# Two linear-attention blocks on one core: the denominators summed by partition copies on ScalarE and additions on VectorE instead of matmuls

## The chip, the core and the metric

The kernel runs on one core of one Trainium2 chip. The metric is the device time of one execution in microseconds; less is better. The engines are named as in the profile: PE is TensorE (PEld its weight loads), ACT is ScalarE, DVE is VectorE, POOL is GpSimd, SP is SyncE, which only issues DMAs. All of them run at the same time, each through its own list of instructions in program order, and semaphores make them wait for one another.

## What is computed

Two blocks, A and B, with their own inputs, do the same work; their outputs stand side by side. For each:

```
qkv = x @ wqkv                      # x: 2048 x 640, wqkv: 640 x 1920, 32 heads of 20
phi(t) = (t + 1 if t > 0 else exp(t)) + 1e-6
pq, pk = phi(q), phi(k)
kv  = einsum("bhsd,bhse->bhde", pk, v)
z   = einsum("bhsd->bhd", pk)
num = einsum("bhqd,bhde->bhqe", pq, kv)
den = einsum("bhqd,bhd->bhq", pq, z) + 1e-6
out = (num / den, heads concatenated) @ wo
```

All of it is fp32. For each token and head, `den` is one number: the sum over the head's 20 dimensions of pq times z.

## The kernel before

**Accuracy.** TensorE multiplies in a reduced fp32 form. Each operand is therefore split into a high part (a copy on ScalarE) and a low part (source minus high part, on VectorE), and a product is three matmuls: high by high, high by low, low by high. A helper `split` issues the copy at once and puts the subtraction on a list; `flush` (called at every slot, see below) issues what is on the list.

**First half (to about 313 us).** It makes phi(k) and, in place of kv, the products of phi(k) with x, from which kv and its product with wo follow (640 x 640, one per block). It is ordered by a small planner in the kernel. The change doesn't touch it.

**Second half.** The 2048 tokens of each block are cut into 4 units of 512 tokens, so there are 8 units (u = 0 to 7). Two stages work on a unit:

- the projection (`qmm`, `qphi`, `qacc`): five column blocks c = 0 to 4 of q, transposed, so that 128 columns of q lie on the partitions and 512 tokens in the free dimension. Each takes 15 matmuls of 512 columns into a bank `psq`. ScalarE takes the exponential (eq, L1092) and the ReLU (rq, L1093) from the bank, VectorE combines them to pq (L1094), and pq times z is added up over the five blocks in `acc` (128 x 512; first block on ScalarE, L1102, the others on VectorE, L1104). The columns of q are ordered by dimension first and head second, so partition p belongs to head p mod 32, and the four groups of 32 partitions of acc still have to be summed.
- the output (`outmm`): 14 steps s = 0 to 13, 108 matmuls of 320 columns. They compute pq/den times the combined 640 x 640 matrix by a scheme with 7 products for each of two halves q of the unit. The products use two banks `pa` and two `pe`, and `psb`. A bank pa is copied out by ScalarE (L1218) after steps 0 and 1, again after 4 and 5, after 8 and 9, and after 10 and 11, and between these the next product is added to the same bank. So the matmuls of step 4 wait for the copy of step 0, and those of step 10 for the copy of step 8.

The stages run in the order q0, q1, o0, q2, o1, q3, ..., q7, o6, o7.

**The denominators before.** `split_acc` splits acc into a high and a low part (ScalarE L918, VectorE L915), `denmm` multiplies both with `same`, a 128 x 128 matrix that is 1 where two partitions belong to the same head (two matmuls of 512 columns, L1114 and L1115, into the bank `psd`). All 128 partitions then hold the sum of their head. `recip` takes the reciprocal on VectorE in two halves of 256 tokens (L1120), and `divide` multiplies one half of pq by it (VectorE, L1126). Then `d_sums` forms sums and differences of parts of pq (sr, L1142 to L1147), and `a_split` and `d_split` split these into the high and low operands of `outmm` (da and ds).

**What sets the order.** It is written out by hand. `run("q", u, c, k)` is called after each three matmuls of the projection and `run("o", u, s)` after each step of the output; `at(slot, f, ...)` puts a function into such a slot. The dict `chain` holds the slots of the denominator's functions for each unit v. Those of unit 0 lie in the projection of unit 1, those of unit v > 0 in the output stage of unit v - 1. As each engine works in program order, a slot decides behind which other instruction a function's instructions stand. In the projection, `qphi` of block c comes after all five slots of that block. In the output, a step's own copies come before its slot. Around the slots stand, among others, the splits of wo of block B (woh and wol, in the projection of unit 1), the rounding of the next x (xqh, L962, slots 4, 6, 8, 10 and 12 of an output stage) and the splits of block B's matrix (fsh, in the output stage of unit 0 and others).

Of the kernel before, what the change touches and what calls it, by code (L numbers as in the profile page):

```python
# [7 lines left out]
F32 = mybir.dt.float32  # L8
BF16 = mybir.dt.bfloat16
F32R = mybir.dt.float32r  # L10
I32 = mybir.dt.int32
AF = mybir.ActivationFunctionType
OP = mybir.AluOpType
# [205 lines left out]
def tile_linear_attn_pair(ctx: ExitStack, tc: tile.TileContext, ins, out: bass.AP):  # L219
    nc = tc.nc  # L220
    P = 128
# [19 lines left out]
    kx, kg, q1a, q1b, q2, q3 = [], [], [], [], [], []  # L241
# [19 lines left out]
    same = base.tile([P, P], F32R)  # L261
# [415 lines left out]
    a, z, x = jh[0][0:P], jl[0][0:P], jr[0][0:P]  # L677
# [117 lines left out]
    for p in range(4, NPB):  # L795
        i, h = divmod(p - 2, 2)
# [9 lines left out]
    for p in range(NPB + 1, NP):  # L806
        if p == NPB + 1:
            fl = kvs
        else:
            i, h = divmod(p - NPB - 2, 2)  # L810
# [70 lines left out]
    for g, (h0, nh) in enumerate(GROUPS):  # L881
        cols = NC * DH * nh
        w = Space("wv", cols, (BD,))
# [17 lines left out]
    def bank(name, tag="one", bufs=3):  # L901
        at, n = ptags[tag]
        pn[tag] = pn.get(tag, -1) + 1
        return psum.tile([P, 512], F32, name=name, tag=f"bank{at + pn[tag] % n}", bufs=1)
# [7 lines left out]
    def flush():  # L912
        while lows:
            lo, src, hi = lows.pop(0)
            nc.vector.tensor_tensor(lo, src, f32(hi), op=OP.subtract)  # L915

    def split(hi, lo, src, now=False):
        nc.scalar.activation(hi, src, AF.Copy)  # L918
        lows.append((lo, src, hi))
        if now:  # L920
            flush()
# [148 lines left out]
    pq, acc, den, dd = {}, {}, {}, {}  # L1070
# [32 lines left out]
        else:  # L1103
            nc.vector.scalar_tensor_tensor(acc[u], p, z, acc[u], op0=OP.mult, op1=OP.add)  # L1104

    def split_acc(u):
        t = q2[0].tile([P, 2, 512], F32R, name="ac", tag="sr", bufs=2)
        split(t[:, 0], t[:, 1], acc.pop(u))
        acc[u] = t

    def denmm(u):
        t = acc.pop(u)
        ps = den.pop(u) if u in den else bank("psd", "small", 1)
        nc.tensor.matmul(ps, same, t[:, 0], start=True, stop=False)  # L1114
        nc.tensor.matmul(ps, same, t[:, 1], start=False, stop=True)  # L1115
        den[u] = (ps, q2[0].tile([P, 512], F32, name="rd", tag="rd", bufs=1))

    def recip(u, h):
        ps, r = den[u]
        nc.vector.reciprocal(r[:, h * 256:(h + 1) * 256], ps[:, h * 256:(h + 1) * 256])  # L1120

    def divide(u, h):

# [4 lines left out]
    da, ds, sr = {}, {}, {}  # L1128
# [161 lines left out]
    h = NG - 1  # L1290
# [8 lines left out]
    for c in range(NC):  # L1299
# [3 lines left out]
        for u in range(1, NU - 1):  # L1303
# [3 lines left out]

    at(("q", 1, 0, 0), z_end)

    den[0] = bank("psd", "small", 1)  # L1310

    chain = {
        0: [(("q", 1, 0, 0), split_acc, 0), (("q", 1, 1, 1), denmm, 0), (("q", 1, 1, 1), recip, 0, 0),
            (("q", 1, 1, 1), recip, 0, 1), (("q", 1, 1, 2), divide, 0, 0), (("q", 1, 1, 4), divide, 0, 1),
            (("q", 1, 2, 0), d_sums, 0, 0), (("q", 1, 2, 2), a_split, 0, 0), (("q", 1, 2, 4), d_sums, 0, 1),
            (("q", 1, 3, 1), d_split, 0, 0), (("q", 1, 3, 4), a_split, 0, 1), (("q", 1, 4, 1), d_split, 0, 1)]}
    for v in range(1, NU):
        w, u = v - 1, v + 1
        if v == NU - 1:
            chain[v] = [(("o", w, 1), split_acc, v), (("o", w, 4), denmm, v), (("o", w, 4), recip, v, 0),  # L1320
                        (("o", w, 5), divide, v, 0), (("o", w, 6), a_split, v, 0, 0), (("o", w, 6), d_sums, v, 0, 0),
                        (("o", w, 7), d_split, v, 0, 0), (("o", w, 8), a_split, v, 1, 0), (("o", w, 8), d_sums, v, 1, 0),
                        (("o", w, 9), recip, v, 1), (("o", w, 10), d_split, v, 1, 0), (("o", w, 12), divide, v, 1),
                        (("o", v, 0), a_split, v, 0, 1), (("o", w, 13), d_sums, v, 0, 1),
                        (("o", v, 0), d_split, v, 0, 1), (("o", v, 2), d_sums, v, 1, 1),
                        (("o", v, 2), a_split, v, 1, 1), (("o", v, 3), d_split, v, 1, 1)]
        elif v == 1:
            chain[v] = [(("o", w, 4), split_acc, v), (("o", w, 7), denmm, v), (("o", w, 8), recip, v, 0),
                        (("o", w, 10), recip, v, 1), (("o", w, 11), divide, v, 0),
                         (("o", w, 12), divide, v, 1), (("q", u, 0, 2), d_sums, v, 0), (("q", u, 0, 4), a_split, v, 0),  # L1330
                         (("q", u, 1, 2), d_sums, v, 1), (("q", u, 2, 1), d_split, v, 0), (("q", u, 3, 1), a_split, v, 1),
                         (("q", u, 3, 4), d_split, v, 1)]
        else:
            chain[v] = [(("o", w, 2), split_acc, v), (("o", w, 5), denmm, v), (("o", w, 7), recip, v, 0),
                        (("o", w, 9), recip, v, 1), (("o", w, 11), divide, v, 0),
                         (("o", w, 12), divide, v, 1), (("q", u, 0, 2), d_sums, v, 0), (("q", u, 0, 4), a_split, v, 0),
                         (("q", u, 1, 2), d_sums, v, 1), (("q", u, 2, 1), d_split, v, 0), (("q", u, 3, 1), a_split, v, 1),
                         (("q", u, 3, 4), d_split, v, 1)]
    for v in range(NU):
        for a, f, *x in chain[v]:  # L1340
            at(a, f, *x)
# [63 lines left out]
```

## Time and profile before

| | us |
|---|---|
| median of 3 runs | 570.86 (570.66 to 571.42) |
| the profiled execution | 570.49 |
| its span, from its first to its last instruction | 568.7 |
| TensorE busy | 564.2 |
| VectorE busy | 434.2 |
| ScalarE busy | 341.4 |

The granted TensorE clock is 1.000 over the span. A row of the timeline reads: start in us, duration in us, engine, line, operation, output tile <- input tiles, shape, how many, and in brackets how long the engine sat idle before it and for whom it waited. A row of a group reads: line, engine, operation, tiles, shape, count, then busy us, mean ns of one, and idle us before them. Matmuls overlap, so the cost of one in a dense stream is the distance of two starts, not its duration.

### The profile page before, as it was taken

Reading aid. Unit: us, or ns where it says so; the run is one execution under the profiler, and the core shown is the slowest. Engines: PE = TensorE matmul, PEld = TensorE weight load, DVE = VectorE, ACT = ScalarE, POOL = GpSimd, SP = SyncE. Lnnn points to the kernel's source line nnn. Section 1 sums busy time; section 2 is a strip of 40 time slices with the busy share of each in tenths; the row PEclk is TensorE's granted clock in tenths of the full one; section 3 lists DMA queues with packets and bytes.
Section 4 is the critical chain, followed back from the end, with each engine's and each line's share of the span. In section 5 each row is a group of like instructions: output and inputs, shape, how many; then the busy total and the mean of one; then the engine's idle time right before and its main releaser. Section 6 shows DMA issues by size and latency. Waiting matters only on the chain.

```text
span 568.7 us, 9488 instructions
## 1 busy us (share of the span) xinstructions
PE 564.2 (99%) x3524; PEld 536.0 (94%) x3524; DVE 434.2 (76%) x706; ACT 341.4 (60%) x619; POOL 62.9 (11%) x103
## 2 busy tenths in 40 slices
PE   9999999999999999999999999999999999999997
PEld 7999999999999999999988899898989989898997
DVE  6888687598888767888645899977788776758792
ACT  6878566673788756766436665646656464644551
POOL 0210011110001021110010103110011201001010
PEclk9999999999999999999999999999999999999999
DMA  8993755758849676697999967662454996122022
GB/s 294 370 283 118 198 150 125 238 142 248 262 116 274 180 190 181 199 295 202 352 281 342 355 238 258 228 193 95 146 202 144 366 391 224 42 76 93 0 93 92
DMA packets 68321, 117.64 MB, mean 207 GB/s; under 512 B 6804, under 2 KB 30132, under 8 KB 68276
## 3 DMA queue, kind: packets, MB, share of 16 engines
q1 hardware_dynamic: 59060, 89.94, 48.0%
q0 software_dynamic: 8928, 26.92, 17.0%
q8 instruction: 27, 0.44, 0.3%
q10 hardware_dynamic: 288, 0.20, 0.1%
q14 instruction: 18, 0.15, 0.1%
HBM read 71.13 MB, written 35.41 MB: 187 GB/s over the span
## 4 chain that ended last, share of the span: by engine, by line
PE 99%; DVE 0%; issue 0%
PE psg L316 25%; PE pa L1203 12%; PE ka L316 10%; PE psq L924 8%; PE psq L926 8%; PE psq L925 8%; PE pe L1203 6%; PE ke L316 5%; PE psk L719 4%; PE psb L1203 4%; PE kb L316 3%; PE pskv L556 1%; PE pskv L984 1%; PE psm L583 1%; PE psi L647 1%; PE psk L696 1%
## 5 line engine op out<-in xcount | busy, mean ns | idle before, releaser
L316 PE MATMUL psg<-pkl,xnh 128*128 128x320 f32 x320 | 98.9, 309 | 0.0
L316 PE MATMUL psg<-pkh,xnh 128*128 128x320 f32 x320 | 98.8, 309 | 0.0
L316 PE MATMUL psg<-pkh,xnl 128*128 128x320 f32 x320 | 98.5, 308 | 0.0
L924 PE MATMUL psq<-xqh,wh 128*128 128x512 f32 x200 | 78.5, 393 | 0.0
L926 PE MATMUL psq<-xqh,wl 128*128 128x512 f32 x200 | 78.0, 390 | 0.0
L925 PE MATMUL psq<-xql,wh 128*128 128x512 f32 x200 | 77.9, 390 | 0.0
L316 PEld LDWEIGHTS psg<-pkl,xnh 128*128 128x128 f32 x320 | 60.1, 188 | 0.0
L316 PEld LDWEIGHTS psg<-pkh,xnl 128*128 128x128 f32 x320 | 60.1, 188 | 0.0
L316 PEld LDWEIGHTS psg<-pkh,xnh 128*128 128x128 f32 x320 | 60.0, 188 | 0.0
L489 ACT ACTIVATE kt<-ka 128x320 f32<-128x320 f32 x52 | 22.7, 437 | 59.1 <-PE ka L316 59.0
L1218 ACT ACTIVATE o<-pa 128x320 f32<-128x320 f32 x64 | 27.9, 438 | 45.2 <-PE pa L1203 45.0
L406 POOL DMA_DIRECT2D zacc<-ek x32 | 26.6, 840 | 236.1 <-DVE ek L499 173.7
L1094 DVE SCALAR_TENSOR_TENSOR pq<-eq,rq 128x512 f32<-128x512 f32 x40 | 27.7, 691 | 30.7 <-ACT rq L1093 30.6
L537 DVE TENSOR_TENSOR gacc<-psg,gacc 128x320 f32<-128x320 f32 x60 | 29.4, 489 | 23.5 <-PE psg L316 22.5
L1092 ACT ACTIVATE eq<-psq 128x512 f32<-128x512 f32 x40 | 23.9, 597 | 36.9 <-PE psq L926 34.8
L926 PEld LDWEIGHTS psq<-xqh,wl 128*128 128x128 f32 x200 | 37.5, 188 | 7.9
L925 PEld LDWEIGHTS psq<-xql,wh 128*128 128x128 f32 x200 | 37.6, 188 | 7.6 <-DMA xql<-xd 0.2
L924 PEld LDWEIGHTS psq<-xqh,wh 128*128 128x128 f32 x200 | 37.6, 188 | 7.1
L401 ACT ACTIVATE pkh<-ek,epst 128x640 fp32r<-128x640 f32 x32 | 26.5, 828 | 6.9 <-DVE ek L499 6.7
L1203 PE MATMUL pa<-fh,dal 128*128 128x320 f32 x96 | 29.7, 309 | 0.0
L1203 PE MATMUL pa<-fh,dah 128*128 128x320 f32 x96 | 29.7, 309 | 0.0
L1203 PE MATMUL pa<-fl,dah 128*128 128x320 f32 x96 | 29.7, 309 | 0.0
(215 smaller groups left out, 1558.2 us busy)
## 6 DMA issues: line engine op xcount, KB each, us to landing
zacc<-ek POOLq DMA_DIRECT2D x32, 320.0 KB, 4.8
xql<-xd SPq DMA_DIRECT2D x40, 256.0 KB, 5.0
xd<-xl SPq DMA_DIRECT2D x29, 320.0 KB, 3.9
out<-o POOLq DMA_DIRECT2D x28, 320.0 KB, 3.6
xns<-in_A_x SPq DMA_DIRECT2D x16, 320.0 KB, 5.4
xts<-in_B_xt_tiles SPq DMA_DIRECT2D x16, 320.0 KB, 3.6
xns<-in_B_x SPq DMA_DIRECT2D x16, 320.0 KB, 5.8
xqs<-in_A_xt SPq DMA_DIRECT2D x20, 256.0 KB, 5.8
```

What stands on the lines that cost most here:

```text
L316: nc.tensor.matmul(o, a.r, w.r, start=start and k == i == 0, stop=k == n - 1 and i == 2, skip_group_check=True)
L401: note("ACT", n + 110, lambda: act(hi.r, p.f, AF.Identity, bias=epst), [hi], [p, K0.all], by=8.0)
L406: note("POOL", 1.0, lambda: nc.gpsimd.dma_start(z.f, p.f, **kw), [z], [p], dma=1.0 if first else 1.86)
L537: tt(o, BK[k].tile[:, :HF], o, op=OP.add)
L719: nc.tensor.matmul(o[h][:, :HF], x[a].r, w[c][h * HF:h * HF + HF].r, start=c == 0 and i == 0, stop=c == NC - 1 and i == 2, skip_group_chec ...
L924: nc.tensor.matmul(o, whi, xhi, start=first, stop=False)
L925: nc.tensor.matmul(o, whi, xlo, start=False, stop=False)
L926: nc.tensor.matmul(o, wlo, xhi, start=False, stop=last)
L1092: nc.scalar.activation(e, ps, AF.Exp)
L1094: nc.vector.scalar_tensor_tensor(pq[u][:, c, :], e, 1.0, r, op0=OP.min, op1=OP.add)
L1203: nc.tensor.matmul(ps, x, y, start=start and n == i == 0, stop=n == len(terms) - 1 and i == 2, skip_group_check=True)
L1218: copy = lambda x, y: nc.scalar.activation(x, y, AF.Copy)
```

## The change

The four partition groups are summed without TensorE. `fold1` copies on ScalarE the upper 64 partitions of the first 256 tokens to the lower 64, and the lower 64 partitions of the last 256 tokens to the upper 64. `fold2` adds them on VectorE: the lower 64 partitions now hold the first 256 tokens, the upper 64 the last 256. `fold3` swaps on ScalarE groups of 32 partitions within each 64 (four copies), `fold4` adds these and takes one reciprocal of 256 columns on VectorE, and `fold5` copies the result on ScalarE to both halves of the partitions (two copies for each 256 tokens). `divide` and all that follows is the same. So there are ten copies, three additions and one reciprocal per unit in place of one copy, one subtraction, two matmuls and two reciprocals. No bank of PSUM is used for it any more. The slots change with it:

```diff
-    def split_acc(u):
-        t = q2[0].tile([P, 2, 512], F32R, name="ac", tag="sr", bufs=2)
-        split(t[:, 0], t[:, 1], acc.pop(u))
-        acc[u] = t
-
-    def denmm(u):
...
-    def recip(u, h):
-        ps, r = den[u]
-        nc.vector.reciprocal(r[:, h * 256:(h + 1) * 256], ps[:, h * 256:(h + 1) * 256])
+    def fold1(u):
+
+        t = q2[0].tile([P, 2, 512], F32, name="ac", tag="sr", bufs=2)
+        a = acc[u]
+        nc.scalar.activation(t[0:64, 0, 0:256], a[64:128, 0:256], AF.Copy)
+        nc.scalar.activation(t[64:128, 0, 0:256], a[0:64, 256:512], AF.Copy)
+        den[u] = t
+
+    def fold2(u):
+        t, a = den[u], acc.pop(u)
+        for p, c in ((0, 0), (64, 256)):
+            rows = slice(p, p + 64)
+            nc.vector.tensor_tensor(t[rows, 0, 256:512], a[rows, c:c + 256], t[rows, 0, 0:256], op=OP.add)
+
+    def fold3(u, h):
+        t = den[u]
+        for p, q in ((0, 32), (32, 0)):
+            p, q = p + 64 * h, q + 64 * h
+            nc.scalar.activation(t[p:p + 32, 1, 0:256], t[q:q + 32, 0, 256:512], AF.Copy)
+
+    def fold4(u):
+        t = den[u]
+        nc.vector.tensor_tensor(t[:, 1, 0:256], t[:, 0, 256:512], t[:, 1, 0:256], op=OP.add)
+        nc.vector.reciprocal(t[:, 1, 256:512], t[:, 1, 0:256])
+        den[u] = (t, q2[0].tile([P, 512], F32, name="rd", tag="rd", bufs=1))
+
+    def fold5(u, h):
+        t, r = den[u]
+        for p in (0, 64):
+            nc.scalar.activation(r[p:p + 64, h * 256:(h + 1) * 256], t[64 * h:64 * h + 64, 1, 256:512], AF.Copy)
...
-        0: [(("q", 1, 0, 0), split_acc, 0), (("q", 1, 1, 1), denmm, 0), (("q", 1, 1, 1), recip, 0, 0),
-            (("q", 1, 1, 1), recip, 0, 1), (("q", 1, 1, 2), divide, 0, 0), (("q", 1, 1, 4), divide, 0, 1),
+        0: [(("q", 1, 0, 0), fold1, 0), (("q", 1, 0, 2), fold2, 0), (("q", 1, 0, 3), fold3, 0, 0),
+            (("q", 1, 0, 4), fold3, 0, 1), (("q", 1, 1, 1), fold4, 0), (("q", 1, 1, 3), fold5, 0, 0),
+            (("q", 1, 1, 4), fold5, 0, 1), (("q", 1, 1, 4), divide, 0, 0), (("q", 1, 2, 0), divide, 0, 1),
...
-            chain[v] = [(("o", w, 1), split_acc, v), (("o", w, 4), denmm, v), (("o", w, 4), recip, v, 0),
-                        (("o", w, 5), divide, v, 0), (("o", w, 6), a_split, v, 0, 0), (("o", w, 6), d_sums, v, 0, 0),
+            chain[v] = [(("o", w, 1), fold1, v), (("o", w, 2), fold2, v), (("o", w, 3), fold3, v, 0),
+                        (("o", w, 3), fold3, v, 1), (("o", w, 4), fold4, v), (("o", w, 6), fold5, v, 0),
+                        (("o", w, 6), divide, v, 0), (("o", w, 7), a_split, v, 0, 0), (("o", w, 7), d_sums, v, 0, 0),
...
-            chain[v] = [(("o", w, 2), split_acc, v), (("o", w, 5), denmm, v), (("o", w, 7), recip, v, 0),
-                        (("o", w, 9), recip, v, 1), (("o", w, 11), divide, v, 0),
...
+            a = (3, 4, 5, 6, 7, 9, 10) if v == 1 else (2, 3, 4, 5, 6, 8, 9)
+            chain[v] = [(("o", w, a[0]), fold1, v), (("o", w, a[1]), fold2, v), (("o", w, a[2]), fold3, v, 0),
+                        (("o", w, a[3]), fold3, v, 1), (("o", w, a[4]), fold4, v), (("o", w, a[5]), fold5, v, 0),
+                        (("o", w, a[6]), fold5, v, 1), (("o", w, 11), divide, v, 0), (("o", w, 12), divide, v, 1),
```

The slots of `divide` for the units 1 to 6 stay where they were, and those of the sums and splits behind it stay for all units but the last, where some move back by one step.

More of the change, by code (lines that the diff above doesn't have):

```diff
@@ L1104, in qacc @@
             nc.vector.scalar_tensor_tensor(acc[u], p, z, acc[u], op0=OP.mult, op1=OP.add)
-    def split_acc(u):
-        t = q2[0].tile([P, 2, 512], F32R, name="ac", tag="sr", bufs=2)
-        split(t[:, 0], t[:, 1], acc.pop(u))
-        acc[u] = t
-    def denmm(u):
[L1112 to L1116, printed above, removed]
-    def recip(u, h):
-        ps, r = den[u]
-        nc.vector.reciprocal(r[:, h * 256:(h + 1) * 256], ps[:, h * 256:(h + 1) * 256])
+    def fold1(u):
[23 more added lines that the diff above has]
+            nc.scalar.activation(r[p:p + 64, h * 256:(h + 1) * 256], t[64 * h:64 * h + 64, 1, 256:512], AF.Copy)
     def divide(u, h):
@@ L1308, in tile_linear_attn_pair @@
     at(("q", 1, 0, 0), z_end)
-    den[0] = bank("psd", "small", 1)
     chain = {
-        0: [(("q", 1, 0, 0), split_acc, 0), (("q", 1, 1, 1), denmm, 0), (("q", 1, 1, 1), recip, 0, 0),
-            (("q", 1, 1, 1), recip, 0, 1), (("q", 1, 1, 2), divide, 0, 0), (("q", 1, 1, 4), divide, 0, 1),
+        0: [(("q", 1, 0, 0), fold1, 0), (("q", 1, 0, 2), fold2, 0), (("q", 1, 0, 3), fold3, 0, 0),
+            (("q", 1, 0, 4), fold3, 0, 1), (("q", 1, 1, 1), fold4, 0), (("q", 1, 1, 3), fold5, 0, 0),
+            (("q", 1, 1, 4), fold5, 0, 1), (("q", 1, 1, 4), divide, 0, 0), (("q", 1, 2, 0), divide, 0, 1),
             (("q", 1, 2, 0), d_sums, 0, 0), (("q", 1, 2, 2), a_split, 0, 0), (("q", 1, 2, 4), d_sums, 0, 1),
@@ L1319, in tile_linear_attn_pair @@
         if v == NU - 1:
-            chain[v] = [(("o", w, 1), split_acc, v), (("o", w, 4), denmm, v), (("o", w, 4), recip, v, 0),
-                        (("o", w, 5), divide, v, 0), (("o", w, 6), a_split, v, 0, 0), (("o", w, 6), d_sums, v, 0, 0),
-                        (("o", w, 7), d_split, v, 0, 0), (("o", w, 8), a_split, v, 1, 0), (("o", w, 8), d_sums, v, 1, 0),
-                        (("o", w, 9), recip, v, 1), (("o", w, 10), d_split, v, 1, 0), (("o", w, 12), divide, v, 1),
+            chain[v] = [(("o", w, 1), fold1, v), (("o", w, 2), fold2, v), (("o", w, 3), fold3, v, 0),
+                        (("o", w, 3), fold3, v, 1), (("o", w, 4), fold4, v), (("o", w, 6), fold5, v, 0),
+                        (("o", w, 6), divide, v, 0), (("o", w, 7), a_split, v, 0, 0), (("o", w, 7), d_sums, v, 0, 0),
+                        (("o", w, 8), d_split, v, 0, 0), (("o", w, 9), a_split, v, 1, 0), (("o", w, 9), d_sums, v, 1, 0),
+                        (("o", w, 10), fold5, v, 1), (("o", w, 10), d_split, v, 1, 0), (("o", w, 12), divide, v, 1),
                         (("o", v, 0), a_split, v, 0, 1), (("o", w, 13), d_sums, v, 0, 1),
@@ L1326, in tile_linear_attn_pair @@
                         (("o", v, 2), a_split, v, 1, 1), (("o", v, 3), d_split, v, 1, 1)]
[L1327 to L1332, printed above, removed]
-        else:
-            chain[v] = [(("o", w, 2), split_acc, v), (("o", w, 5), denmm, v), (("o", w, 7), recip, v, 0),
-                        (("o", w, 9), recip, v, 1), (("o", w, 11), divide, v, 0),
-                         (("o", w, 12), divide, v, 1), (("q", u, 0, 2), d_sums, v, 0), (("q", u, 0, 4), a_split, v, 0),
-                         (("q", u, 1, 2), d_sums, v, 1), (("q", u, 2, 1), d_split, v, 0), (("q", u, 3, 1), a_split, v, 1),
-                         (("q", u, 3, 4), d_split, v, 1)]
+        else:
+            a = (3, 4, 5, 6, 7, 9, 10) if v == 1 else (2, 3, 4, 5, 6, 8, 9)
+            chain[v] = [(("o", w, a[0]), fold1, v), (("o", w, a[1]), fold2, v), (("o", w, a[2]), fold3, v, 0),
+                        (("o", w, a[3]), fold3, v, 1), (("o", w, a[4]), fold4, v), (("o", w, a[5]), fold5, v, 0),
+                        (("o", w, a[6]), fold5, v, 1), (("o", w, 11), divide, v, 0), (("o", w, 12), divide, v, 1),
+                        (("q", u, 0, 2), d_sums, v, 0), (("q", u, 0, 4), a_split, v, 0), (("q", u, 1, 2), d_sums, v, 1),
+                        (("q", u, 2, 1), d_split, v, 0), (("q", u, 3, 1), a_split, v, 1),
+                        (("q", u, 3, 4), d_split, v, 1)]
     for v in range(NU):
```

## The prediction

> **What bounds the kernel now.** I read the page's busy shares and its chain first.
>
> ```profile
> span 568.7 us, 9488 instructions
> ...
> PE 564.2 (99%) x3524; PEld 536.0 (94%) x3524; DVE 434.2 (76%) x706; ACT 341.4 (60%) x619; POOL 62.9 (11%) x103
> ...
> PE 99%; DVE 0%; issue 0%
> ```
>
> TensorE (PE) works through the whole span, and the chain that ended last is TensorE to 99%. So a matmul that goes is time that goes, as long as TensorE finds its next operand and its next free bank ready. And a wait on TensorE is never won back, because it has no idle time later. VectorE (DVE, 76%) and ScalarE (ACT, 60%) have room on average, but the average doesn't say whether they have it where the change puts its work. The profiled execution took 570.49 us, 1.8 us more than its span; the median of the three runs, 570.86, lies 0.37 above it. I make the sum as a difference on the profiled execution and add it to the median.
>
> **What goes.** The view of the tiles psd, ac and rd has the old denominators:
>
> ```profile
> L1114 PE MATMUL psd<-ac,same x8: 391/399/399, 318.1 to 537.3; 128*128 128x512 f32 x8
> L1115 PE MATMUL psd<-ac,same x8: 389/393/466, 318.3 to 537.5; 128*128 128x512 f32 x8
> L918 ACT ACTIVATE ac<-acc x8: 622/632/634, 316.9 to 535.7; 128x512 fp32r<-128x512 f32 x8
> L915 DVE TENSOR_TENSOR ac<-acc,ac x8: 686/692/693, 317.6 to 536.4; 128x512 fp32r<-128x512 f32 x8
> L1120 DVE RECIPROCAL rd<-psd x16: 1696/1748/1758, 320.4 to 546.2; 128x256 f32<-128x256 f32 x16
> ```
>
> Sixteen matmuls of 0.39 us would be 6.3 us, but a duration is not what a matmul costs: the next starts before it ends. The cost is the distance of starts, from the timeline of TensorE:
>
> ```profile
> 349.13 0.40 PE L924 MATMUL psq<-xqh,wh 128*128 128x512 f32 x1
> ...
> 366.16 0.31 PE L1203 MATMUL pa<-fh,dah 128*128 128x320 f32 x1
> ...
> 382.46 0.40 PE L924 MATMUL psq<-xqh,wh 128*128 128x512 f32 x1
> ```
>
> From 349.13 to 366.16 lie the 75 matmuls of one projection stage: 17.03/75 = 0.227 us each. The output stage up to 382.46 holds 108 matmuls of 320 columns and one pair for a denominator: (16.30 - 0.45)/108 = 0.147. So a pair is worth 0.45 us, and eight pairs 3.6 us.
>
> Per unit VectorE loses the subtraction (0.69) and two reciprocals (3.5) and gets three additions and one reciprocal of 256 columns. ScalarE loses one copy of 512 columns and gets ten of 256.
>
> **What the new instructions cost.**
>
> ```profile
> L918 ACT ACTIVATE dah<-pq 128x256 fp32r<-128x256 f32 x7 | 2.9, 416 | 0.0
> L915 DVE TENSOR_TENSOR dal<-pq,dah 128x256 fp32r<-128x256 f32 x7 | 2.9, 418 | 0.0
> ...
> 394.59 0.42 ACT L918 ACTIVATE dah<-pq 128x256 fp32r<-128x256 f32 x1
> ...
> 394.90 1.06 ACT L918 ACTIVATE dsh<-sr 128x1024 fp32r<-128x1024 f32 x1
> ...
> L962 ACT ACTIVATE xqh<-xqs 128x512 fp32r<-128x512 f32 x34 | 21.0, 624 | 0.0
> L918 ACT ACTIVATE fsh<-wst 128x640 fp32r<-128x640 f32 x5 | 3.7, 736 | 0.8 <-DVE wst L1022 0.8
> L1218 ACT ACTIVATE o<-pa 128x320 f32<-128x320 f32 x64 | 27.9, 438 | 45.2 <-PE pa L1203 45.0
> ```
>
> A copy of 256 columns takes 0.42 us on ScalarE, and the next independent instruction starts 0.31 after it (394.59 to 394.90), 0.1 before it ends. An addition takes 0.42. No row shows a copy that moves data to other partitions, nor one of 32 or 64 partitions; these rows are the nearest, and I take 0.42, with 0.31 and 0.52 (a quarter to either side) as ends.
> The Trainium skill (ScalarE: Activation LUTs, What ACT_TABLE_LOAD costs) gives a copy with immediate scale and bias 186 ns plus 0.833 ns a column, 399 ns here, and an overlap of some 93 ns. By that the whole sum would come out some 0.1 us lower.
>
> VectorE per unit: 4.2 us before, 3 x 0.42 + 1.75 = 3.0 after. ScalarE: 0.6 before, ten starts of 0.31 = 3.1 after. That alone would be harmless. But the new chain crosses between the two engines four times, both work strictly in program order here, and what stands behind a waiting fold waits too. So I walked through the places where TensorE has little margin, with the durations above.
>
> **Unit 0, where the margin is nothing.** Its denominators are worked out during the projection of unit 1:
>
> ```profile
> 316.11 0.75 DVE L1104 SCALAR_TENSOR_TENSOR acc<-pq,z,acc 128x512 f32<-128x512 f32 x1
> 316.89 0.63 ACT L918 ACTIVATE ac<-acc 128x512 fp32r<-128x512 f32 x1 [1.55 <-DVE acc L1104]
> 317.43 1.35 ACT L918 ACTIVATE woh<-wo 80x640 fp32r<-80x640 f32 x2
> 318.19 1.55 DVE L915 TENSOR_TENSOR wol<-wo,woh 80x640 fp32r<-80x640 f32 x2
> 318.69 0.58 ACT L1092 ACTIVATE eq<-psq 128x512 f32<-128x512 f32 x1
> 319.16 0.58 ACT L1093 ACTIVATE rq<-psq 128x512 f32<-128x512 f32 x1
> 319.77 0.69 DVE L1094 SCALAR_TENSOR_TENSOR pq<-eq,rq 128x512 f32<-128x512 f32 x1
> 320.38 3.36 DVE L1120 RECIPROCAL rd<-psd 128x256 f32<-128x256 f32 x2
> 323.66 1.43 DVE L1126 SCALAR_TENSOR_TENSOR pq<-pq,rd 128x1280 f32<-128x1280 f32 x1
> ...
> 326.40 0.69 DVE L1094 SCALAR_TENSOR_TENSOR pq<-eq,rq 128x512 f32<-128x512 f32 x1
> ...
> 327.80 0.68 DVE L1142 TENSOR_TENSOR sr<-pq 128x512 f32<-128x512 f32 x1
> ...
> 320.00:328.00 8.00, 8.00 (x40) 6.74 (x39) 7.96 (x8) 4.79 (x10) 1.18 (x2) 1.00 1.01 356
> ...
> 335.74 0.78 ACT L1218 ACTIVATE o<-pa 128x320 f32<-128x320 f32 x2
> ...
> 336.24 0.42 PE L1203 MATMUL pa<-fh,dsh 128*128 128x320 f32 x1
> ```
>
> The row of the stretch from 320 to 328 us (PE, PEld, DVE, ACT, POOL busy) has VectorE busy for 7.96 of 8 us: here it is full. At 335.74 ScalarE, which comes late behind this backlog, copies the first product out of the bank pa, and at 336.24 TensorE adds to that bank again. That matmul shows 0.42 in place of 0.31: it already waits, by some 0.1. What comes later on VectorE here comes later on TensorE.
>
> Now the new order, hops of 0.03 between engines (316.86 to 316.89). ScalarE: fold1 at 316.89 and 317.20, woh at 317.51 and 318.13. VectorE: the first wol waits for its woh, 318.27, and fold2 stands behind it: 319.00 and 319.32. ScalarE: four fold3 copies from 319.45, the last at 320.38, and only then, in its order, the exponential of unit 1: 320.69 in place of 318.69. So pq comes at 321.77, 2.0 us later than before. fold4 starts at 322.38, its reciprocal at 322.83, until 324.58. ScalarE's four fold5 copies run from 324.61 to 325.85, and the next exponential and ReLU behind them until 326.92. VectorE waits for fold5, divides at 325.37, makes pq at 326.95 and its acc, and divides the second half at 328.33; the sums (sr) start at 329.82 in place of 327.80. The shorter VectorE work is used up by its waits for ScalarE: the 2.0 us stay. From there on the work is that of before and VectorE has no gap to catch up in, so the copy of 335.74 comes at 337.74 and TensorE's matmul of 336.24 at 338.24: **+2.0 us**. The pair that unit 0 loses is inside this wait.
>
> Then unit 1, in the output stage of unit 0:
>
> ```profile
> 339.23 0.63 ACT L918 ACTIVATE ac<-acc 128x512 fp32r<-128x512 f32 x1 [0.84 <-DVE acc L1104]
> ...
> 342.72 0.44 ACT L1218 ACTIVATE o<-pa 128x320 f32<-128x320 f32 x1 [0.43 <-PE pa L1203]
> ...
> 343.84 0.31 PE L1203 MATMUL pa<-fh,dah 128*128 128x320 f32 x1
> ```
>
> The tightest pair of each output stage is step 8's copy of pa (342.72 to 343.16) and step 10, which writes pa (343.84): 0.68 us of margin. The acc of unit 1 is 2.0 us later too, so ScalarE gets on at 341.23 and has before that copy: six fold copies (1.9), two copies of pa (0.7), two xqh (1.0) and a form's split (0.6), each less its overlap: 4.2. The copy runs from 345.44 to 345.88; step 10 would start at 338.24 + 7.60 - 0.45 = 345.39. A wait of **0.55 us**, less the pair of unit 1, **-0.45**.
>
> Units 2 to 6: acc is in time, and fold3 and fold4 are done before step 8, in the 2 to 3 us that ScalarE idles there. Two fold5 copies (0.62) stand between steps 8 and 9 and delay the copy of step 9 by some 0.2 of its 0.68. Nothing reaches TensorE: five pairs, **-2.27**.
>
> Unit 7, whose folds stand close together:
>
> ```profile
> 535.69 0.63 ACT L918 ACTIVATE ac<-acc 128x512 fp32r<-128x512 f32 x1 [0.43 <-DVE acc L1104]
> ...
> 539.70 1.49 DVE L1126 SCALAR_TENSOR_TENSOR pq<-pq,rd 128x1280 f32<-128x1280 f32 x1
> ...
> 542.96 0.42 ACT L1218 ACTIVATE o<-pa 128x320 f32<-128x320 f32 x1
> ...
> 543.88 0.31 PE L1203 MATMUL pa<-fh,dah 128*128 128x320 f32 x1
> ```
>
> fold1 at 535.69, fold2 at 536.14, four fold3 until 537.94, fold4 and the reciprocal until 540.17, two fold5 until 540.93: the divide starts at 540.96 in place of 539.70 and ends at 542.45. Behind it ScalarE splits (0.5) and copies step 8's pa from 543.0 to 543.44, and step 10 would start at 543.88 - 0.45 = 543.43: a wait of **0.1**, less the pair, **-0.45**.
>
> Sum: 2.0 + 0.55 - 0.45 - 2.27 + 0.1 - 0.45 = -0.5 us: 570.0 for the profiled execution, **570.3** on the median. With the copy at 0.31 it is 1.7 less (ten copies on unit 0's path, six on unit 1's, whose wait then vanishes), 568.6. A measurement of this kernel tells apart about 0.2%, 1.14 us. So I forecast no measurable change.
>
> **Rivals.**
> *TensorE never waits.* All of the 3.6 us and the old 0.1 come back: 567.1. For it speaks that VectorE has 1.2 us less to do per unit, and that TensorE shows no wait after 337 us now. Against it speaks that in unit 0 the chain hops between engines while VectorE is full, and that the margin at 336.24 is used up. Chance 0.15.
>
> *The copies are dearer, and ScalarE's order becomes the bound: slower.* Each 0.1 us on a copy's price costs 1.0 in unit 0 (ten on the path), 0.6 in unit 1 (six) and 0.7 in unit 7 (one fold1, four fold3, two fold5, no margin left), 2.3 in all. From 0.49 us a copy the kernel is measurably slower; at 0.52 it is 572.6. A hidden cost of moving between partition groups, or waits by the whole tile rather than its part, would do this. Against it: no copy of that width shows more than 0.42. Chance 0.18.
>
> *The clock falls.* Two waits of 2.5 and 0.55 us in one stage could put TensorE back into the state in which it starts:
>
> ```profile
> 1.00 4.45 PE L647 MATMUL psi<-idle 128*128 128x512 bf16 x10 [1.00 <-DVE ones L324]
> ```
>
> Ten matmuls of 512 columns took 4.45 us there, 0.2 each above the 0.227 of later. Paid again once, that is 2.2 us: 572.5. Against it, no wait of the trace comes close, so it shows nothing either way. The Trainium skill (TensorE: Matmul & The Clock Gate, What's actually happening) halves the clock only after an idle window of about 3.4 us; by that rule these waits don't suffice. Chance 0.05.
>
> **How the numbers follow.** The forecast's case has 0.62: its own range, 568.6 to 572.0, reaches from the cheaper copy to one at 0.49, and I split it 0.09 faster, 0.48 same, 0.05 slower. The first rival is all faster (0.15); the second is 0.02 same and 0.16 slower; the third 0.02 and 0.03. Together 0.24 faster, 0.52 same, 0.24 slower. The range from 567.8 to 572.7 leaves out most of the first rival and what lies beyond the second, less than 2 in 10.
>
> **What would show it.** In the new profile: no psd; ScalarE's copies with 32 and 64 partitions at 0.40 to 0.43 us; the exponential of unit 1 near 320.7; the second divide of unit 0 behind pq, near 328.3; a gap on TensorE of about 2.5 us between steps 2 and 4 of the first output stage and one of about 0.5 before its step 10; after 347 us TensorE without gaps, and projection and output stage together 32.9 us instead of 33.3. I am wrong if there is no gap at 336 to 338 us, if the copies take 0.5, or if later stages have gaps too.

## The result and the profile after

The changed kernel takes 574.34 us (573.56 to 574.75, 6 runs) against 571.09 us of the kernel before (570.34 to 571.46, 6 runs): a ratio of 1.0057, 95% interval 1.0044 to 1.0070. It is 3.2 us slower. All medians of the kernel before, in the later sections too, are those of its fast runs; one run of 1442.86 us is left out. The profiled execution took 573.56 us, with a span of 571.8 against 568.7.

The head of its page (span, then busy time and share of each engine), and the granted clock of TensorE in 40 slices:

```profile
span 571.8 us, 9534 instructions
...
PE 562.4 (98%) x3508; PEld 533.2 (93%) x3508; DVE 427.2 (75%) x714; ACT 369.9 (65%) x691; POOL 62.9 (11%) x103
...
PEclk9999999999999999999999999999999999999999
```

TensorE has 16 matmuls fewer and is busy for 1.8 us less, but it now waits in places where it didn't. The clock is full in every slice. VectorE is busy for 7 us less (the forecast's 1.2 a unit would be 9.6) and ScalarE for 28.5 us more. Who TensorE waited for from 300 us on (waiting line, releaser, total us, times, longest); in the kernel before this answer has no row there:

```profile
PE pa L1218 <- ACT o L1233: 2.1, 3, 1.4
PE pe L1218 <- DVE dsl L915: 1.7, 1, 1.7
PE pa L1218 <- DVE dal L915: 0.6, 1, 0.6
PE psm L925 <- DVE wol L915: 0.4, 1, 0.4
```

The same waits in TensorE's timeline (start, duration), each as the last matmul before it and the first after it:

```profile
332.98 0.30 PE L1218 MATMUL pa<-fl,dah 128*128 128x320 f32 x1
333.93 0.42 PE L1218 MATMUL pa<-fh,dal 128*128 128x320 f32 x1 [0.64 <-DVE dal L915]
...
335.65 0.31 PE L1218 MATMUL pe<-fl,dsh 128*128 128x320 f32 x1
337.66 0.41 PE L1218 MATMUL pe<-fh,dsl 128*128 128x320 f32 x1 [1.70 <-DVE dsl L915]
...
339.08 0.31 PE L1218 MATMUL pe<-fh,dsl 128*128 128x320 f32 x1
339.76 0.42 PE L1218 MATMUL pa<-fh,dsh 128*128 128x320 f32 x1 [0.37 <-ACT o L1233]
...
346.77 0.31 PE L1218 MATMUL pa<-fh,dal 128*128 128x320 f32 x1
348.45 0.41 PE L1218 MATMUL pa<-fh,dah 128*128 128x320 f32 x1 [1.37 <-ACT o L1233]
...
546.17 0.31 PE L1218 MATMUL pa<-fh,dal 128*128 128x320 f32 x1
546.88 0.42 PE L1218 MATMUL pa<-fh,dah 128*128 128x320 f32 x1 [0.40 <-ACT o L1233]
```

Starts lie 0.147 us apart in the dense stream. I count as a wait what is above that, and with it the 0.10 by which the matmul behind a released one starts late too. That is 0.9, 2.0 and 0.6 us in steps 0 to 4 of the first output stage, 1.6 before its step 10, and 0.7 in the output stage of unit 6 (two more of 0.2 in those of units 2 and 3 and the one of the psm matmul, 0.6, aren't shown). Together they are 6.8 us; less 3.6 for the eight pairs and the old wait of 0.1 that leaves +3.1, the difference of the spans. The large ones are in the places of the forecast, but they are larger. Where the time comes from is seen on ScalarE and VectorE in the projection of unit 1:

```profile
317.05 0.42 ACT L1110 ACTIVATE ac<-acc 64x256 f32<-64x256 f32 x1 [1.55 <-DVE acc L1104]
317.48 0.42 ACT L1111 ACTIVATE ac<-acc 64x256 f32<-64x256 f32 x1
317.90 1.37 ACT L918 ACTIVATE woh<-wo 80x640 fp32r<-80x640 f32 x2
319.42 0.86 DVE L1118 TENSOR_TENSOR ac<-acc,ac 64x256 f32<-64x256 f32 x2
319.86 0.42 ACT L1124 ACTIVATE ac<-ac 32x256 f32<-32x256 f32 x1 [0.59 <-DVE ac L1118]
321.58 0.60 ACT L1092 ACTIVATE eq<-psq 128x512 f32<-128x512 f32 x1
322.70 0.69 DVE L1094 SCALAR_TENSOR_TENSOR pq<-eq,rq 128x512 f32<-128x512 f32 x1 [1.56 <-ACT rq L1093]
325.55 1.72 ACT L1135 ACTIVATE rd<-ac 64x256 f32<-64x256 f32 x4 [0.66 <-DVE ac L1129]
331.32 0.69 DVE L1157 TENSOR_TENSOR sr<-pq 128x512 f32<-128x512 f32 x1
339.27 0.77 ACT L1233 ACTIVATE o<-pa 128x320 f32<-128x320 f32 x2
```

Each copy takes 0.42 us, as forecast. But the second fold1 starts 0.43 after the first, the split of wo 0.42 after that, the four fold5 copies take 1.72 together, and from the first fold3 (319.86) to the exponential behind the fourth (321.58) it is 1.72 too. In the forecast these were 0.31 apart. This execution runs 0.15 us behind that of before already at 286 us (286.85 against 286.71, the first projection's first matmul), before any change; less that, the exponential comes 2.7 us late, the sums (331.32) 3.4 and the copy of pa (339.27) 3.4, where the forecast had 2.0 for each. VectorE, which had no idle time over 0.06 us here before, now waits for ScalarE four times between 317 and 329 us, 3.9 us in all.

### The profile page after: what moved, and what is told of

It reads as the page before. It is cut to its first block, busy times and chain, and to the rows that moved or that the text cites. A ratio compares the mean times of both kernels' runs of the same rounds, so it can differ in the third digit from the quotient of the medians.

```text
span 571.8 us, 9534 instructions
## 1 busy us (share of the span) xinstructions
PE 562.4 (98%) x3508; PEld 533.2 (93%) x3508; DVE 427.2 (75%) x714; ACT 369.9 (65%) x691; POOL 62.9 (11%) x103
```

## Experiments

The theory: the forecast's chain is right and one price is wrong. An instruction of ScalarE or VectorE whose partitions start elsewhere than those of the one before starts only when that one has ended, so a fold copy costs 0.43 us and not 0.31. The rivals were that moving data across partitions is dear, that the number of crossings between the engines makes the loss whatever a copy costs, and that it is spread over all units.

### The price by itself

Series of six independent instructions behind the end of the kernel. A triple is the first partition of the output, that of the input, and the number of partitions; the series run as copies on ScalarE, then as additions and as copies on VectorE.

```diff
+    sp = [stage(f"p{i}") for i in range(7)]
+    for t in sp:
+        nc.vector.memset(t, 1.0)
...
+    pats = [[(0, 0, 128)] * 6, [(0, 0, 64)] * 6, [(0, 64, 64)] * 6, [(0, 0, 64), (64, 64, 64)] * 3,
+            [(0, 64, 64), (64, 0, 64)] * 3, [(0, 0, 64), (64, 0, 64)] * 3, [(0, 0, 64), (0, 64, 64)] * 3,
+            [(0, 0, 32)] * 6]
...
+            dst = sp[1 + i % 6][o:o + w, 0:256]
+            src = sp[0][a:a + w, 0:256]
+                nc.scalar.activation(dst, src, AF.Copy)
```

> The changed kernel with series of six independent copies (256 columns) on ScalarE, additions and copies on VectorE, appended behind its last output, when these engines have nothing else to do; each series has its own pattern of partitions. Theory (an instruction that starts at other partitions than the one before it starts only when that one has ended): starts 0.31 us apart on ScalarE in all series in which neither input nor output changes its first partition, also in the one that moves data from partitions 64-127 to 0-63 each time; 0.42 to 0.44 apart in those in which the first partition of the input, of the output or of both alternates. VectorE the same, 0.33 to 0.35 against 0.43 to 0.45 for additions. Rival (moving data between partitions is what costs): 0.42 in the series that moves each time from 64 to 0, 0.31 in the one that alternates between 0 to 0 and 64 to 64 without moving. Second rival (fewer than 128 partitions cost the overlap): 0.42 in all series with 64 or 32 partitions.

The timeline of the series, two rows of each (start, duration; with "x2" the row takes in the next one too, and rows of neighbouring windows overlap). ScalarE: 64 partitions from 0 to 0; from 64 to 0 each time; alternating between 0 to 0 and 64 to 64:

```profile
574.66 0.70 ACT L1372 ACTIVATE p<-p 64x256 f32<-64x256 f32 x2
574.97 0.70 ACT L1372 ACTIVATE p<-p 64x256 f32<-64x256 f32 x2
...
576.63 0.70 ACT L1372 ACTIVATE p<-p 64x256 f32<-64x256 f32 x2
576.94 0.70 ACT L1372 ACTIVATE p<-p 64x256 f32<-64x256 f32 x2
...
578.71 0.41 ACT L1372 ACTIVATE p<-p 64x256 f32<-64x256 f32 x1
579.15 0.42 ACT L1372 ACTIVATE p<-p 64x256 f32<-64x256 f32 x1
```

The starts are 0.31 us apart in the first two and 0.44 in the third, although the second moves data across partitions each time and the third never does. The series in which only the output or only the input alternates are 0.44 apart as well (583.53 to 583.97, 586.17 to 586.61), and 32 partitions with one start 0.31. So it is neither the move nor the number of partitions: it is the change of the first partition from one instruction to the next, on either side. The next instruction then starts 0.02 to 0.03 us after the end of the one before. VectorE, additions without a change and with one of input and output together (either alone wasn't run there):

```profile
591.61 0.74 DVE L1374 TENSOR_TENSOR p<-p 64x256 f32<-64x256 f32 x2
591.95 0.75 DVE L1374 TENSOR_TENSOR p<-p 64x256 f32<-64x256 f32 x2
...
595.54 0.42 DVE L1374 TENSOR_TENSOR p<-p 64x256 f32<-64x256 f32 x1
595.99 0.42 DVE L1374 TENSOR_TENSOR p<-p 64x256 f32<-64x256 f32 x1
```

0.34 against 0.45; VectorE's copies of the same size last 0.29 and start 0.20 or 0.32 apart. The Trainium skill (VectorE: DVE Perf Modes, Two Vector instructions with no wait between them) states this for VectorE: an instruction whose input or output starts in another group of 32 partitions than the last one used is held until the earlier ones have finished. VectorE's rows agree, with 0.45 in place of 0.34. ScalarE's show the same behaviour.

### The copies at the price that was forecast

```diff
-        nc.scalar.activation(t[0:64, 0, 0:256], a[64:128, 0:256], AF.Copy)
-        nc.scalar.activation(t[64:128, 0, 0:256], a[0:64, 256:512], AF.Copy)
+        nc.scalar.activation(t[0:64, 0, 0:128], a[64:128, 0:128], AF.Copy)
+        nc.scalar.activation(t[64:128, 0, 0:128], a[0:64, 256:384], AF.Copy)
...
-            nc.scalar.activation(t[p:p + 32, 1, 0:256], t[q:q + 32, 0, 256:512], AF.Copy)
+            nc.scalar.activation(t[p:p + 32, 1, 0:128], t[q:q + 32, 0, 256:384], AF.Copy)
...
-            nc.scalar.activation(r[p:p + 64, h * 256:(h + 1) * 256], t[64 * h:64 * h + 64, 1, 256:512], AF.Copy)
+            nc.scalar.activation(r[p:p + 64, h * 256:h * 256 + 128], t[64 * h:64 * h + 64, 1, 256:384], AF.Copy)
```

The divide, not shown here, reads one column of the reciprocals for all 256 and lasts 1.49 us, as in the changed kernel.

> The ten copies per unit take 128 columns in place of 256, so that starts lie 0.31 us apart without any overlap; the additions, the reciprocal and the divide keep their sizes by reading columns twice. The denominators of half the tokens are not worked out. Theory (the forecast failed only in the copies' distance of 0.43 in place of 0.31): the time comes down to that of before, +0.0 to +0.8 us against it (some 571.1 to 571.9), TensorE's waits in the first output stage fall from 4.4 to about 3.3 us, those before step 10 in the output stages of units 2, 3 and 6 vanish. Rival (the number of crossings between the engines makes the loss, not the price of a copy): still over +2 us, waits as in the changed kernel.

570.88 us against 571.13, ratio 1.0001 (0.9991 to 1.0010): the whole loss is gone, with the same number of instructions and crossings. TensorE's waits from 300 us on:

```profile
PE pe L1222 <- DVE dsl L915: 1.7, 1, 1.7
PE pa L1222 <- ACT o L1237: 1.1, 2, 0.7
PE psm L925 <- DVE wol L915: 0.2, 1, 0.2
```

These are nearly the forecast's waits: 2.6 us in steps 2 to 4 of the first output stage and, with the late start behind it, 1.0 before step 10 (forecast: 2.5 and 0.55), and none in later stages. The copies come out a little cheaper than forecast, since the last of a group also ends after 0.31 and not 0.42.

### Which unit

> Unit 0's denominators by matmuls as before, units 1 to 7 by folds as in the change. Theory: the waits of the psm matmul (0.6 us) and of steps 0 to 4 of the first output stage (3.5 us) go, the one before its step 10 stays at about 1.4, small ones in the stages of units 2 and 3 and 0.5 to 0.7 in that of unit 6: 7 pairs of 0.45 saved against 2.3 of waits, -0.9 us against before (570.2), 4 us less than the changed kernel. Rival (the loss is spread over all units): at least half of the change's +3.2 us stays.

The functions and slots of the denominators as before for unit 0 alone, the folds for the others: 570.69 us against 571.13, ratio 0.9991 (0.9982 to 1.0000). Of the change's loss 3.7 us are gone. What TensorE still waits for from 300 us on:

```profile
PE pa L1234 <- ACT o L1249: 1.8, 2, 1.4
```

I had expected -0.9, and it is -0.4: the wait before step 10 is 1.6 us with the late start behind it, not 1.4, and the others come to 1.1 (0.7 and two of 0.2), so seven pairs (3.15) leave 0.45. The opposite, folds for unit 0 alone:

> Only unit 0's denominators by folds, units 1 to 7 by matmuls: the part of the change that the theory holds for most of the loss, alone. Theory: the psm matmul and steps 0 to 4 of the first output stage wait 4.2 us in all, one pair and the old wait of 0.1 are saved: +3.4 us against before (574.5). Rival (the parts work together, and unit 0 alone finds room): +1.5 or less.

574.59 us against 571.20, ratio 1.0060 (1.0045 to 1.0075): unit 0 alone costs +3.4 us, all of the loss. The rest of the change comes out about even. Its waits:

```profile
PE pe L1234 <- DVE dsl L915: 1.7, 1, 1.7
PE pa L1234 <- DVE dal L915: 0.6, 1, 0.6
PE psm L925 <- DVE wol L915: 0.4, 1, 0.4
PE pa L1234 <- ACT o L1249: 0.4, 1, 0.4
```

And with units 0, 1 and 7 by matmuls, 2 to 6 by folds:

> Units 0, 1 and 7 by matmuls as before, units 2 to 6 by folds. Theory: five pairs of 0.45 saved, waits only of 0.2 each in the output stages of units 2 and 3: -1.9 us against before (569.2). Rival (a pair of matmuls in the stream is worth less than the distance of starts says): between -0.9 and 0.

569.87 us against 571.13, ratio 0.9976 (0.9967 to 0.9986): 1.4 us less by the ratio, 0.8 to 1.9 by its interval, where 1.9 was expected. The trace has no wait but the two of 0.2, and each of its output stages with folds and without a wait lasts 15.84 us in place of 16.30, as the theory has it. The second half of the profiled execution, from the first projection's first matmul on, took 280.2 us against 282.0 before, 1.8 less. Its first half, which no edit touches, took 0.9 us longer (287.62 against 286.71); whether the median carries such a difference isn't shown. Some 0.3 of the missing 0.5 lies outside the spans: this kernel's executions last 2.1 us longer than their spans, those of the kernel before 1.8. Why is open.

### Unit 0's copies on VectorE

```diff
+    def move(u, o, x):
+        if u == 0:
+            nc.vector.tensor_copy(o, x)
+        else:
+            nc.scalar.activation(o, x, AF.Copy)
```

All copies of the folds call it, and the other units have the slots of the next experiment.

> As with the moved slots, but unit 0 by folds too, its ten copies on VectorE (0.29 us each, 0.32 apart when partitions change) in place of ScalarE: no crossings between the engines in unit 0's chain. Theory (in unit 0 VectorE is full, so what comes later or longer on it arrives on TensorE): 3.2 us of copies there against 1.2 us less of the rest leave some 2 to 2.5 us of waits in the first output stage, less one pair: -0.5 to -1.2 us against before. Rival (only the crossings cost): no wait at steps 0 to 4, -3.6 us.

570.03 us against 571.20, ratio 0.9981 (0.9972 to 0.9991), -1.1 us. There is no crossing left among unit 0's folds, and still TensorE waits in the first output stage:

```profile
PE pe L1224 <- DVE dsl L915: 1.7, 1, 1.7
PE pa L1224 <- ACT o L1239: 0.4, 1, 0.4
PE pa L1224 <- DVE dal L915: 0.2, 1, 0.2
```

So the loss doesn't hang on the crossings alone. Unit 0 by folds costs 2.1 us here (-1.1 against the -3.2 of the next experiment, which differs in unit 0 only), and 3.4 with the copies on ScalarE. The stretch from 317 to 338 us (PE, PEld, DVE, ACT, POOL busy), in the changed kernel and in this one:

```profile
317.00:338.00 21.00, 18.25 (x88) 14.97 (x87) 16.72 (x25) 15.84 (x30) 1.18 (x2) 1.00 0.85 299
317.00:338.00 21.00, 19.06 (x92) 15.65 (x91) 20.30 (x36) 10.79 (x19) 1.18 (x2) 1.00 0.91 318
```

In the changed kernel VectorE waits for ScalarE there. In this one it has no idle time over 0.06 us between two instructions, so what bounds the place is VectorE's own work, the copies among it.

### The folds where there is room for them

```diff
-        0: [(("q", 1, 0, 0), fold1, 0), (("q", 1, 0, 2), fold2, 0), (("q", 1, 0, 3), fold3, 0, 0),
+        0: [(("q", 1, 0, 0), split_acc, 0), (("q", 1, 1, 1), denmm, 0), (("q", 1, 1, 1), recip, 0, 0),
...
-                        (("o", w, 6), divide, v, 0), (("o", w, 7), a_split, v, 0, 0), (("o", w, 7), d_sums, v, 0, 0),
-                        (("o", w, 8), d_split, v, 0, 0), (("o", w, 9), a_split, v, 1, 0), (("o", w, 9), d_sums, v, 1, 0),
+                        (("o", w, 6), divide, v, 0), (("o", w, 8), a_split, v, 0, 0), (("o", w, 7), d_sums, v, 0, 0),
+                        (("o", w, 9), d_split, v, 0, 0), (("o", w, 9), a_split, v, 1, 0), (("o", w, 9), d_sums, v, 1, 0),
...
-            a = (3, 4, 5, 6, 7, 9, 10) if v == 1 else (2, 3, 4, 5, 6, 8, 9)
+            a = (5, 6, 10, 10, 10, 12, 12, 12, 13) if v == 1 else (2, 3, 4, 5, 6, 10, 10, 11, 12)
```

The list `a` also gives unit 1's two divides later slots (12 and 13), and the lines above it give unit 7's first two splits slots that are later by one.

> Unit 0 by matmuls, units 1 to 7 by folds, with other slots: unit 1's folds in slots 5, 6, 10, 10, 10, 12, 12 with the divides in 12 and 13, so that the copy of step 8 stands in front of eight of them; units 2 to 6 with both fold5 in slot 10; unit 7's first splits one slot later, behind the copy of step 8. Theory (what is left of the loss in units 1 to 7 is only folds standing on ScalarE in front of the copies that free pa): no wait of TensorE after 337 us, seven pairs of 0.45 saved: -3.2 us against before, 567.9. Rival (ScalarE or VectorE has not the time for the folds, the waits appear elsewhere): -0.5 us as with the old slots, with waits at other steps.

568.05 us against 571.20, ratio 0.9944 (0.9931 to 0.9956): 3.2 us less than before, as expected, and 6 us less than the changed kernel. The span, and two rows of the view by stretches (PE, PEld, DVE, ACT and POOL busy), one projection and one output stage:

```profile
span 565.2 us, 9529 instructions
...
348.45:365.49 17.04, 17.04 (x77) 14.09 (x76) 16.34 (x22) 12.98 (x23) 4.70 (x10) 1.00 0.57 186
365.49:381.33 15.84, 15.84 (x109) 15.84 (x108) 11.79 (x19) 11.60 (x26) 2.96 (x6) 1.00 0.81 277
```

The output stage lasts 15.84 us in place of 16.30 (366.16 to 382.46 before): a pair is worth the 0.45 that the distances said. The view of waits has no row for TensorE from 300 us on.

## Why the prediction was wrong

The forecast was 570.3 us and no measurable change; the range ended at 572.7, and 574.3 was measured.

**The step that failed** is the price of a copy: "the next independent instruction starts 0.31 after it (394.59 to 394.90), 0.1 before it ends". Those two rows are both on all 128 partitions. A fold copy starts on other partitions than its neighbour, and then the next one starts 0.43 to 0.44 after it. The duration, 0.42, was right; the overlap was carried over from rows that didn't have what is new in the folds, a change of the first partition. I had put 0.52 at the upper end for a hidden cost of moving between groups, but as a duration with the same 0.1 of overlap. What was measured, 0.43 to 0.44 with none, amounts to a copy of some 0.53 to 0.55 in that reckoning, beyond that end. With the copies' price brought back by half the columns, the +3.2 us of the change become +0.0. So the price makes 3.2 of the 3.7 us between the forecast's difference (-0.5) and the measured one, and the forecast's other sums were short by 0.5.

**The terms.** Unit 0: +2.0 forecast, +3.4 measured, with the ten copies that the forecast counted on the path: 10 x 0.12 = 1.2 of the 1.4 missing. With half the columns it is +2.3. Unit 1: a wait of 0.55 forecast, 1.6 measured; six copies give 0.7 more. The wait of half the copies' size, 1.0, shows that the forecast's sum there was short by some 0.4 as well. Units 2 to 6: none forecast, two of 0.2 measured. There fold5 stands between the copies of steps 8 and 9, where the forecast allowed a delay of 0.2 of a margin of 0.68; with fold5 moved to slot 10, and nothing else moved for these units, both waits are gone. What makes these two stages worse than the others is read from the trace, not tested: in the output stage of unit 2 ScalarE also has splits of wq around these copies, and in that of unit 3 a split of fsh stands in the same place (the copies of pa are those of steps 8 and 9):

```profile
446.32 0.44 ACT L1233 ACTIVATE o<-pa 128x320 f32<-128x320 f32 x1 [0.81 <-PE pa L1218]
446.66 0.46 ACT L918 ACTIVATE fsh<-t 128x320 fp32r<-128x320 f32 x1
...
447.54 0.83 ACT L1135 ACTIVATE rd<-ac 64x256 f32<-64x256 f32 x2
448.40 0.44 ACT L1233 ACTIVATE o<-pa 128x320 f32<-128x320 f32 x1
```

In the output stage of unit 4 there is no such split, and no wait. Unit 7: 0.1 forecast, 0.7 measured; seven copies give 0.8. Pairs: 0.45 each, right in every stage without a wait.

**What was right.** The places and their order: the wol behind its woh, unit 0's exponential behind fold3, the full VectorE, the matmul at step 4 with no margin, step 8's copy in front of step 10. With the price brought back to the forecast's (half the columns) the time is that of before, +0.0, against the forecast's -0.5: unit 0 and unit 1 cost 0.3 and 0.45 more than forecast there, unit 7 0.1 less.

**The rivals.** That TensorE never waits was wrong for the reasons named. That the copies are dearer was the one that happened, and its place was right, though not the cause that it named first: moving between partition groups costs nothing, changing the first partition does. Its 0.18 was too little, because I let the price vary by a quarter where the overlap could go altogether. Its 572.6 was too small for other reasons too: at 0.53 to 0.55 its own rate of 2.3 us for each 0.1 gives 572.8 to 573.3, and the two waits of 0.2, the 0.5 of the other sums and a kernel before that measured 0.2 higher (571.09 against 570.86) make up the rest. That the clock falls did not happen. The granted clock is 1.00 through waits of 1.9 us, and the matmuls behind the longest one start 0.15 apart as before (337.91 to 338.05). A longer idle time did it: in the run with the series, the last matmul ends at 568.8 us, and the granted clock is 1.00 from 572 to 573 us and 0.50 from 574 to 575. The Trainium skill's window of about 3.4 us (TensorE: Matmul & The Clock Gate, What's actually happening) fits both, without being tested more closely by them.

## What to carry to other kernels

On an engine that is always busy, work that is taken off pays by the distance of starts, and it pays only where the replacement isn't on the way to that engine; here the same replacement, in the right slots, was worth -0.45 us a unit in seven places and cost 3.4 us in the eighth. Price a new instruction by a row that shares its partitions with its neighbours as the new one will, not only by a row of the same size. And look in the engine's own order at what stands behind each new instruction: moving the folds (and two divides and two splits with them) behind the copies that free a bank took the waits of units 1 to 7 from 2.7 us to none.

## What the runs showed of the hardware

On ScalarE, copies of 256 columns start 0.31 us apart as long as input and output keep their first partition, and 0.44 apart when either changes; on VectorE it is 0.34 without and 0.45 with a change of both for additions, 0.20 and 0.32 for copies. Moving data from partitions 64 to 127 down to 0 to 63 costs nothing more than copying it in place, 0.31 us from start to start on ScalarE and 0.34 (additions) on VectorE both ways. Partitions count for nothing in the price: 32, 64 or 128 of them take the same 0.40 to 0.42 us on ScalarE. An idle time of 1.9 us on TensorE left its granted clock at 1.00; some 5 us after its last matmul the clock was 0.50.
